# Batch 0's first pair of heads: later queries turned by DMA instead of by TensorE, with a new order of all steps

## The chip, the cores and the metric

The kernel runs on one core of a Trainium2 chip. Its engines work side by side, each through its own list of instructions in order: TensorE (PE in the profile; its weight loads are PEld), VectorE (DVE), ScalarE (ACT), GpSimd (POOL) and SyncE (SP), which issues DMA transfers. They wait for one another by semaphores. The metric is the device time of one execution in microseconds, as the median of the runs.

## The reference

Attention with routing, followed by a two-layer MLP. There are 4 batches, 8 heads, 768 positions and 64 columns to a head. Each query and each key is assigned to that one of its head's 16 centroids to which it has the greatest cosine. A query sees only the keys with its own centroid:

```python
q_assign = np.argmax(np.einsum('bhsd,hcd->bhsc', q_n, c_n), axis=-1)
k_assign = np.argmax(np.einsum('bhsd,hcd->bhsc', k_n, c_n), axis=-1)
mask = q_assign[:, :, :, None] == k_assign[:, :, None, :]
scores = scale * np.matmul(q, k.transpose(0, 1, 3, 2))
scores = np.where(mask, scores, -1000000000.0)
```

A softmax over the keys and a product with `v` follow. The heads are put side by side to rows of 512, and `x @ w_in` (to 2048), `h * sigmoid(h)` and `@ w_out` (back to 512) give the output, 3072 x 512 in float32.

## The kernel before

**Heads and tiles.** Heads are handled in pairs (`p` from 0 to 3), positions in six tiles of 128. Batch 0 runs in two rounds: the first two query tiles of all heads (`NA` = 2, 256 queries), then the other four (512 queries). Batches 1 to 3 run whole. The MLP runs in nine units (`mlp`): batch 0 in three of two tiles, the other batches in two of three tiles each.

**A part** (`part`, line 477 on) prepares tiles of queries and keys for the score matmul. Rows are rounded to fp16 (`hi`, lines 530 to 534) and the remainder kept as a second fp16 (`lo`, line 538). Then the tiles are turned, so that columns lie on partitions; TensorE multiplies them with the centroids (`logits`), the maximum is sought, and a 0/1 code of 16 columns marks the centroid. The code, turned as well, stands as 16 more rows under the 64 rows of values in the buffer `ab`. A score matmul (line 804) takes all 80 rows, so that masked scores come out far below the others.

There are two routes for a part. By TensorE (`turn` is a pair of engines): line 573 transposes values and remainders, 128 columns at once, eight tiles to a bank, and an engine evicts them to `lt` (lines 588, 590); logits take two matmuls to a tile (lines 618 and 622, `twin`); the code is compared out of the logits on VectorE (lines 668, 693), put next to the fp16 rows, transposed by line 573 once more (80 columns), and evicted to `ab` (lines 584, 586). By DMA (`turn` is "DMA"): SyncE issues a DMA transpose (line 553) straight into `ab`; logits take one matmul of 32 columns to a tile (line 627); VectorE adds the two halves (line 644) and finds the maximum (664), GpSimd subtracts it (676), VectorE marks (703, 705) and flips in blocks of 32 (718), and four copies, one for each group of 32 partitions, place the code in `ab` (line 735, `PUTB` names the engine for each group). In the kernel before all of batch 0 goes by TensorE, batches 1 to 3 go by DMA.

**Attention and MLP.** A head's scores go through the exponential on ScalarE (line 811), then line 832 multiplies with V (`vt`, cast by lines 418 to 422), and VectorE normalizes (845, 850). The result is transposed to `xt` by DMA (869) or by TensorE (880). The MLP's first matmul is line 910, tanh 916 on ScalarE, the gate 921 on VectorE, the second matmul 945, then an eviction to `ot` (958 on ScalarE, 960 on VectorE) and the store (963).

**The order.** Every piece of work is a `step` with an engine, a duration that the program assumes, what it depends on, the buffers it takes, and a key. `Plan.order` goes through the steps in assumed time: the step that can start earliest goes next, at equal times that with the lowest key. The outcome is the list of instructions of each engine. Assumed times only make the order; on the chip each instruction waits for the data that it needs. Numbers at the head of the kernel shape the keys and delays: `AT` gives the due times of the rounds and batches, `ML` those of the MLP units, `LEADS` how far ahead of its due time a part's key lies, `REST`, `RLOAD` and `SOON` after which head a part or a load may be placed, `PW` after which event a piece of the MLP's weights is fetched on GpSimd's queue, `DONE`, `WSL`, `FLIP` and `LATE` how much later than assumed something lands. `VC`, `TK`, `TQ`, `TR`, `TS`, `HI`, `HR`, `XT` and `EVAC` name the engine of a kind of work by pair, chunk or unit. Line 356 issues matmuls on zeros into assumed gaps of TensorE until the assumed time `UNREAD`, and up to `MORE` beyond a gap of over 400 ns.

Of the kernel before, what the change touches and what calls it, by code (L numbers as in the profile page):

```python
# [33 lines left out]
class Plan:  # L34
# [14 lines left out]
    def step(self, eng, w, fn, after=(), use=(), key=0.0, load=None, hold=0.0, pace=None, flip=False, lag=None, slack=0.0, port=False):  # L49
        s = Step()  # L50
        s.eng, s.w, s.fn, s.key, s.load, s.hold, s.flip = eng, w, fn, key, load, hold, flip
        s.lag = self.LAG.get(eng, 0) if lag is None else lag
        s.slack = slack
        s.port = port or eng == "POOL"
        s.use = list(use)
        s.n = len(self.steps)
        flat = []

        def gather(a):
            if isinstance(a, (list, tuple)):  # L60
                for x in a:
                    gather(x)
            elif a is not None:
                flat.append(a)

        gather(list(after))
        gather(pace)
        s.after = list({id(x): x for x in flat}.values())
        s.start = s.end = None
        for b in s.use:  # L70
            b.left += 1
        self.steps.append(s)
        return s
# [125 lines left out]
def kernel(  # L199
# [80 lines left out]
    def buf(name):  # L280
        return Buf(pools[name])
# [15 lines left out]

    SMALL = 30
    ISSUE = 470
    PW = [11, 5, 7, 13, 12, 27, 17, 2, 21, 10, 14, 19]  # L300
    UNREAD = 80000.0
    COLD = 8500.0
    MORE = 250.0
    LATE = 900
    FLIP = 1500
    DONE = 600
    WSL = 1000
    AT = [32.0, 63.0, 91.3, 118.4, 233.2, 272.8]
    ML = [55.5, 113.0, 73.2, 121.1, 198.2, 239.3, 267.5, 305.4, 257.3, 449.1]
    PUTB = ["POOL", "POOL", "POOL", "POOL"]  # L310
    VC = ["ACT", "ACT", "POOL", "ACT"]
    VB = "POOL"
    TK = ["ACT", "ACT", "DVE", "DVE", "DVE"]
    TQ = ["DVE", "ACT", "DVE", "DVE", "DVE"]
    TR = ["ACT", "DVE", "DVE", "DVE"]
    TS = ["ACT", "DVE", "DVE", "DVE"]
    HI = ["ACT", "ACT", "ACT", "POOL"]
    HR = ["DVE", "POOL", "DVE", "POOL"]
    LEADS = [27.5, 133.1, 361.9]
    REST = [3, 6, 3, 11]  # L320
    RLOAD = [2, 0, 3, 0]
    SOON = [7, 5, 7, 4]
    XT = ["DVE", "ACT", "ACT", "DVE"]
    EVAC = ["DVE", "DVE", "DVE", "ACT", "ACT", "ACT", "DVE", "ACT", "ACT", "ACT"]
    SPARE = 0
    FINE = 2

# [31 lines left out]

    plan.filler = (pools["M"], lambda t: 180.0 if t < COLD else 112.0, unread, UNREAD, MORE)  # L360

# [22 lines left out]
    def load_q(b, p, key, j0=0, j1=NJ, eng="SP", hs=(0, 1), pace=None):  # L384
        if (b, p) not in nqs:
            nqs[b, p] = buf("nq")
        x = nqs[b, p]

        def f():
            e = nc.sync if eng == "SP" else nc.scalar  # L390
            h0, h1 = 2 * p + hs[0], 2 * p + hs[-1] + 1
            e.dma_start(T["nq"][x.i][:, hs[0] : hs[-1] + 1, j0 * D : j1 * D], rows(q, b, h0, h1, j0, j1))

        s = step(eng, ISSUE, f, use=[x], key=key, load=110 * (j1 - j0) * len(hs), pace=pace, slack=LATE if b else 300 if eng == "ACT" else 0)
        for h in hs:
            for j in range(j0, j1):
                ld_q[b, p, h, j] = s
        return s
# [3 lines left out]
    def load_v(b, p, key, pace=None):  # L402
        eng = VC[p] if b == 0 else VB
        x = buf("nv")

        def f():
            nc.sync.dma_start(T["nv"][x.i], rows(v, b, 2 * p, 2 * p + 2, 0, NJ))

        s = step("SP", ISSUE, f, use=[x], key=key, load=1310, pace=pace, slack=LATE if b else 0)
        for h in range(2):  # L410
            y = buf("vt")
            vts[b, 2 * p + h] = y

            def g(h=h, y=y):
                dst = T["vt"][y.i][:, 0 : NJ * VW].rearrange("p (j c) -> p j c", c=VW)[:, :, 0:D]
                src = T["nv"][x.i][:, h, :].rearrange("p (j d) -> p j d", d=D)
                if eng == "ACT":
                    nc.scalar.copy(dst, src)
                else:
                    (nc.gpsimd if eng == "POOL" else nc.vector).tensor_copy(dst, src)  # L420

            w = {"POOL": pool_w(384), "ACT": act_w(384), "DVE": dve_w(384, 0.55)}[eng]

            cast_v[b, 2 * p + h] = step(eng, w, g, port=eng == "DVE", after=[s, s_ones], use=[x, y], key=key + 20)
# [52 lines left out]
    def part(b, p, segs, a0, due, lead=20.0, hi_eng="POOL", turn="DMA", twin=False, sub="POOL", code_eng=None, pace=None, wait=None):  # L477
# [238 lines left out]
        if turn == "DMA":  # L716
# [8 lines left out]
            for g in range(4):  # L725
# [14 lines left out]
                load = 10 * n if code_eng[g] == "SP" else None  # L740
                placed.append(step(code_eng[g], w, put, after=[s_flip, s_log], use=[ohT, A], key=key + 13 * span, load=load, port=code_eng[g] == "DVE", lag=Plan.LAG.get(code_eng[g], 0) + DONE))

# [229 lines left out]
    def weight(kind, n, event):  # L972

        x, use, name = event

        def f():
            nc.gpsimd.tensor_copy(pace, T[name][use.i][:, D : D + 1])
            if kind == "in":
                nc.gpsimd.dma_start(
                    win_s[:, :, ts(n, 512)], moe_w_in.rearrange("(r p) f -> p r f", p=128)[:, :, ts(n, 512)]  # L980
                )
            else:
                nc.gpsimd.dma_start(
                    wout_s[:, 2 * n : 2 * n + 2, :],
                    moe_w_out[256 * n : 256 * n + 256, :].rearrange("(c p) d -> p c d", p=128),
                )

        return step("POOL", 840, f, after=[x], use=[use], key=-1, load=2450 if kind == "in" else 1220, slack=WSL)


    want = {(n, h): AT[n] + (AT[n + 1] - AT[n]) * h / H for n in range(NU + B - 1) for h in range(H)}

# [13 lines left out]
    engines = dict(twin=True, sub="DVE")  # L1006
    for h in range(2):
        part(
            0, 0, [("k", h, 0, NJ), ("q", h, 0, NA)], (NJ + NA) * h, want[0, h], lead=LEADS[0], hi_eng=HI[0],
            turn=(TK[h], TQ[h]), wait=s_split if h else None, **engines,  # L1010
        )
    for p in range(1, NP):
        part(
            0, p, [("k", 0, 0, NJ), ("k", 1, 0, NJ), ("q", 0, 0, NA), ("q", 1, 0, NA)], 0, want[0, 2 * p], lead=LEADS[0],
            hi_eng=HI[p], turn=(TK[1 + p], TQ[1 + p]), wait=s_cent, **engines,
        )
# [3 lines left out]
    def at(place, f):  # L1020
        todo.setdefault(place, []).append(f)

    for p in range(NP):
        at(RLOAD[p], lambda s, p=p: load_q(0, p, want[1, 2 * p] - 30, NA, NJ, pace=s))
        at(
            REST[p],
            lambda s, p=p: part(
                0, p, [("q", 0, NA, NJ), ("q", 1, NA, NJ)], 2 * (NJ + NA), want[1, 2 * p], lead=LEADS[1], pace=s,
                hi_eng=HR[p], turn=(TR[p], TS[p]), **engines,
            ),  # L1030
        )
    for b in range(1, B):
        for p in range(NP):
# [3 lines left out]
            for f, early in ((load_k, 32), (load_q, 31), (load_v, 30)):  # L1037
                at(place - (SOON[0] if soon else SOON[1]), lambda s, b=b, p=p, f=f, due=due - early: f(b, p, due, pace=s))
            for i in range(2):
                at(  # L1040
                    place + i - (SOON[2] if soon else SOON[3]),
                    lambda s, b=b, p=p, i=i: part(
                        b, p, [("k", i, 0, NJ), ("q", i, 0, NJ)], 12 * i, want[b + NU - 1, 2 * p + i], lead=LEADS[2], pace=s, code_eng=PUTB
                    ),
                )
    for place in range(H * (B + NU - 1)):
        n, h = divmod(place, H)
        per = (AT[n + 1] - AT[n]) / H
        if n < NU:
# [7 lines left out]
    for n in range(4):  # L1057
        w_in_done.append(weight("in", n, events[PW[n]]))
    for n in range(8):
        w_out_done.append(weight("out", n, events[PW[4 + n]]))  # L1060
    units = [(0, *r) for r in UNITS] + [(b, 3 * c, 3 * c + 3) for b in range(1, B) for c in range(2)]
    for n, (b, j0, j1) in enumerate(units):
        mlp(b, j0, j1, ML[n], ML[n + 1], lambda t, n=n: EVAC[n], n == len(units) - 1)

# [31 lines left out]
```

## Time and profile before

| what | value |
|---|---|
| median of the runs | 304.36 us (304.25 to 304.38, 3 runs) |
| the profiled execution | 305.28 us, of it span 303.5 us |
| TensorE busy | 297.6 us |
| ScalarE busy | 226.2 us |
| VectorE busy | 196.6 us |
| GpSimd busy | 118.7 us |

Times in the profile are microseconds from the start of the span unless marked ns. A row of a group gives line, engine, operation, output and input, shapes, count, then busy time and mean of one, then the engine's idle time just before and who ended it. Busy times of groups overlap, since matmuls are pipelined: what a matmul costs on the engine is the distance between starts.

### The profile page before, as it was taken

The page shows a single profiled execution, that of the slowest core. Times are in us where ns is not written, and L with a number is a line of the kernel's source. Part 1 is how long each engine was busy: PE and PEld are TensorE (multiplying, and loading weights), DVE is VectorE, ACT ScalarE, POOL GpSimd, SP SyncE. Part 2 cuts the span into 40 slices and gives each one's busy share as a digit, 9 for nine tenths or more (in the row PEclk, how much of TensorE's full clock was granted, in tenths as well). Part 3 has the DMA queues.
Part 4 walks back from the last instruction along what each step waited for, and adds up shares of the span by engine and source line. Part 5 has one row for each costly group of instructions (what it writes and reads, how often), then busy time and mean ns, then how long its engine had stood idle before and what let it go on. Part 6 is the DMA issues. An engine that isn't in the chain of part 4 may idle for free.

```text
span 303.5 us, 8340 instructions
## 1 busy us (share of the span) xinstructions
PE 297.6 (98%) x3257; PEld 196.9 (65%) x3257; DVE 196.6 (65%) x484; ACT 226.2 (75%) x470; POOL 118.7 (39%) x242
## 2 busy tenths in 40 slices
PE   8999999999999999999999999999999999999995
PEld 6998777658867746666566655766656665555444
DVE  5999687888867946697567962688601686364020
ACT  5869999949899936988779867899888964253221
POOL 3346333497644677367377360464320000000000
PEclk9999999999999999999999999999999999999999
DMA  7999969977579966773968663854403000101211
GB/s 229 304 252 251 207 96 202 201 217 183 116 167 167 235 121 228 164 186 74 248 134 222 91 165 105 247 51 78 81 35 95 5 0 2 69 0 38 88 50 69
DMA packets 68695, 41.53 MB, mean 137 GB/s; under 512 B 48048, under 2 KB 65712, under 8 KB 68656
## 3 DMA queue, kind: packets, MB, share of 16 engines
q1 hardware_dynamic: 63952, 36.64, 50.4%
q0 software_dynamic: 4288, 4.20, 8.7%
q8 instruction: 25, 0.41, 0.6%
q10 hardware_dynamic: 416, 0.16, 0.2%
q14 instruction: 14, 0.11, 0.1%
HBM read 27.30 MB, written 6.29 MB: 111 GB/s over the span
## 4 chain that ended last, share of the span: by engine, by line
PE 94%; DMA 3%; ACT 1%; DVE 0%; issue 0%; ACTq 0%
PE bank L910 27%; PE bank L945 26%; PE bank L804 19%; PE bank L832 11%; PE bank L573 3%; DMA ab<-hl 3%; PE bank L627 2%; PE bank L356 2%; ACT P L811 1%; PE bank L618 1%; PE bank L622 1%; PE bank L880 1%; ACT lt L588 0%; DVE ot L960 0%; ACT ot L958 0%
## 5 line engine op out<-in xcount | busy, mean ns | idle before, releaser
L811 ACT ACTIVATE P<-bank 128x512 f16<-128x512 f32 x288 | 160.2, 650 | 25.7 <-PE bank L804 24.6
L945 PE MATMUL bank<-wout_s,gq 128*128 128x512 f16 (+1 forms) x400 | 100.2, 370 | 0.0
L910 PE MATMUL bank<-xt,win_s 128*128 128x384 f16 (+1 forms) x576 | 96.8, 308 | 0.0
L921 DVE SCALAR_TENSOR_TENSOR gq<-tn,bank 128x384 f16<-128x384 f32 (+1 forms) x144 | 69.4, 503 | 39.3 <-ACT tn L916 36.4
L804 PE MATMUL bank<-ab 80*128 80x256 f16 (+1 forms) x384 | 92.8, 326 | 0.0
L916 ACT ACTIVATE tn<-bank 128x384 f32<-128x384 f32 (+1 forms) x144 | 67.9, 498 | 24.1 <-PE bank L910 22.8
L910 PEld LDWEIGHTS <-win_s 128*128 128x128 f16 x576 | 54.7, 97 | 28.6
L735 POOL COPY ab<-ohT 16x384 f16<-16x384 f16 x96 | 51.5, 536 | 27.6 <-DVE ohT L718 13.5
L945 PEld LDWEIGHTS <-gq 128*128 128x128 f16 x400 | 37.3, 98 | 30.4
L832 PEld LDWEIGHTS <-P 128*128 128x128 f16 x1152 | 46.0, 97 | 12.0 <-ACT P L811 0.8
L832 PE MATMUL bank<-vt,P 128*128 128x65 f16 x1152 | 50.4, 193 | 0.6 <-ACT P L811 0.6
L804 PEld LDWEIGHTS <-ab 80*128 80x128 f16 x384 | 35.0, 97 | 21.9 <-issue 0.2
L676 POOL TENSOR_TENSOR Df<-L,mx 128x192 f32<-128x192 f32 x24 | 13.2, 549 | 40.7 <-DVE mx L664 37.7
L538 DVE SCALAR_TENSOR_TENSOR hl<-nk,hl 128x384 f16<-128x384 f32 (+1 forms) x29 | 19.2, 665 | 6.7 <-POOL hl L534 6.6
L958 ACT COPY ot<-bank 128x512 f32<-128x512 f32 (+1 forms) x16 | 8.9, 558 | 18.0 <-PE bank L945 17.9
L644 DVE TENSOR_REDUCE L<-bank 128x192 f32<-128x384 f32 x24 | 13.2, 551 | 13.4 <-PE bank L627 12.2
L538 DVE SCALAR_TENSOR_TENSOR hl<-nq,hl 128x384 f16<-128x384 f32 (+3 forms) x33 | 19.9, 602 | 0.9 <-POOL hl L534 0.9
L850 DVE TENSOR_TENSOR xn<-bank,rz 128x384 f16<-128x384 f32 (+2 forms) x40 | 19.0, 475 | 1.2
L845 DVE RECIPROCAL rz<-bank 128x6 f32<-128x6 f32 (+2 forms) x40 | 7.2, 180 | 17.1 <-PE bank L832 9.7
L534 POOL TENSOR_SCALAR hl<-nk 128x384 f16<-128x384 f32 (+1 forms) x25 | 13.8, 554 | 10.9 <-PE bank L573 8.7
L534 POOL TENSOR_SCALAR hl<-nq 128x384 f16<-128x384 f32 (+2 forms) x27 | 14.1, 524 | 1.5 <-DMA nq<-in_q_dram 1.4
L718 DVE STREAM_TRANSPOSE ohT<-oh 128x384 f16<-128x384 f16 x24 | 13.8, 576 | 0.8
(60 smaller groups left out, 180.6 us busy)
## 6 DMA issues: line engine op xcount, KB each, us to landing
nv<-in_v_dram SPq DMA_DIRECT2D x16, 384.0 KB, 5.4
out_dram<-ot SPq DMA_DIRECT2D x23, 256.0 KB, 2.1
nk<-in_k_dram SPq DMA_DIRECT2D x15, 384.0 KB, 4.2
nq<-in_q_dram SPq DMA_DIRECT2D x12, 384.0 KB, 4.6
wout_s<-in_moe_w_out_dram POOLq DMA_DIRECT2D x8, 256.0 KB, 7.0
win_s<-in_moe_w_in_dram POOLq DMA_DIRECT2D x4, 512.0 KB, 9.4
nq<-in_q_dram SPq DMA_DIRECT2D x4, 256.0 KB, 6.4
nk<-in_k_dram SPq DMA_DIRECT2D x2, 192.0 KB, 2.6
```

The costliest lines, as they stand in the source:

```text
L534: nc.gpsimd.tensor_scalar(out=dh, in0=src, scalar1=qs, scalar2=1.0, op0=ALU.mult, op1=ALU.mult)
L538: nc.vector.scalar_tensor_tensor(out=dl, in0=src, scalar=qs, in1=dh, op0=ALU.mult, op1=ALU.subtract)
L718: nc.vector.transpose(T["ohT"][ohT.i][:, 0:n, :].rearrange("p n c -> p (n c)"), T["oh"][oh.i][:, 0:n, :].rearrange("p n c -> p (n c)"),)
L735: nc.gpsimd.tensor_copy(dst, src)
L804: nc.tensor.matmul(banks[sb.i][:, at : at + 128 * (c1 - c0)], ab[0:80, kt[j], :], ab[0:80, qt + c0 : qt + c1, :].rearrange("p n c -> p (n ...
L811: nc.scalar.activation(out=T["P"][P.i][:, 0:at], in_=banks[sb.i][:, 0:at], func=AF.Exp, bias=0.0, scale=ESC if b else -ESC)
L832: nc.tensor.matmul(banks[O.i][:, (D + 1) * t : (D + 1) * t + nn], w, vt[:, VW * j : VW * j + nn], start=(j == 0), stop=(j == NJ - 1), skip ...
L850: nc.vector.tensor_tensor(out=T["xn"][xn.i][:, 0:nq, (h % 2) * D : (h % 2) * D + D], in0=banks[O.i][:, 0 : (D + 1) * nq].rearrange("p (t c ...
L910: nc.tensor.matmul(banks[bank.i][:, 0:n], win_s[:, r, ts(fb, 128)], T["xt"][xtb[b].i][:, r, 128 * j0 : 128 * j1], start=(r == 0), stop=(r ...
L916: nc.scalar.activation(out=T["tn"][tn.i][:, 0:n], in_=banks[bank.i][:, 0:n], func=AF.Tanh, bias=0.0, scale=1.0)
L921: nc.vector.scalar_tensor_tensor(out=T["gq"][g.i][:, fb % 4, 0:n], in0=T["tn"][tn.i][:, 0:n], scalar=1.0, in1=banks[bank.i][:, 0:n], op0=A ...
L945: nc.tensor.matmul(banks[bank.i][:, 0 : c1 - c0], T["gq"][gqs[fc // 4].i][:, fc % 4, ts(t, 128)], wout_s[:, fc, c0:c1], start=(fc == 0), s ...
```

## The change

The later 512 queries of batch 0's first pair of heads (8 tiles) go by the DMA route, as the parts of batches 1 to 3 do: `RT` chooses the route for each pair. Their code is placed by `PUTB`, as theirs is, and there the second partition group now goes by a DMA on SyncE's queue in all DMA-routed parts. All numbers that shape the order and most choices of engines are others. The zeros end at 45 us of assumed time and no longer go beyond a gap.

```diff
-    PW = [11, 5, 7, 13, 12, 27, 17, 2, 21, 10, 14, 19]
-    UNREAD = 80000.0
+    PW = [9, 6, 8, 11, 5, 26, 13, 2, 17, 4, 19, 22]
+    UNREAD = 45000.0
     COLD = 8500.0
-    MORE = 250.0
+    MORE = 0.0
     LATE = 900
     FLIP = 1500
-    DONE = 600
-    WSL = 1000
-    AT = [32.0, 63.0, 91.3, 118.4, 233.2, 272.8]
-    ML = [55.5, 113.0, 73.2, 121.1, 198.2, 239.3, 267.5, 305.4, 257.3, 449.1]
-    PUTB = ["POOL", "POOL", "POOL", "POOL"]
-    VC = ["ACT", "ACT", "POOL", "ACT"]
+    DONE = 400
+    WSL = 300
+    AT = [-10.9, 71.7, 88.1, 238.0, 366.9, 396.1]
+    ML = [-113.1, 222.5, 30.1, 200.9, 344.0, 390.7, 161.9, 493.0, 360.6, 591.5]
+    PUTB = ["POOL", "SP", "POOL", "POOL"]
+    VC = ["DVE", "POOL", "DVE", "POOL"]
     VB = "POOL"
-    TK = ["ACT", "ACT", "DVE", "DVE", "DVE"]
-    TQ = ["DVE", "ACT", "DVE", "DVE", "DVE"]
-    TR = ["ACT", "DVE", "DVE", "DVE"]
-    TS = ["ACT", "DVE", "DVE", "DVE"]
-    HI = ["ACT", "ACT", "ACT", "POOL"]
-    HR = ["DVE", "POOL", "DVE", "POOL"]
-    LEADS = [27.5, 133.1, 361.9]
-    REST = [3, 6, 3, 11]
-    RLOAD = [2, 0, 3, 0]
-    SOON = [7, 5, 7, 4]
+    TK = ["DVE", "ACT", "ACT", "DVE", "DVE"]
+    TQ = ["DVE", "ACT", "ACT", "ACT", "DVE"]
+    TR = ["DVE", "DVE", "DVE", "DVE"]
+    TS = ["ACT", "DVE", "ACT", "DVE"]
+    RT = ["DMA", "PE", "PE", "PE"]
+    HI = ["POOL", "ACT", "POOL", "ACT"]
+    HR = ["ACT", "DVE", "DVE", "DVE"]
+    LEADS = [459.5, 76.9, 362.1]
+    REST = [1, 2, 6, 12]
+    RLOAD = [0, 0, 0, 8]
+    SOON = [5, 5, 5, 5]
     XT = ["DVE", "ACT", "ACT", "DVE"]
-    EVAC = ["DVE", "DVE", "DVE", "ACT", "ACT", "ACT", "DVE", "ACT", "ACT", "ACT"]
+    EVAC = ["ACT", "DVE", "DVE", "ACT", "DVE", "ACT", "ACT", "ACT", "ACT", "ACT"]
...
                 0, p, [("q", 0, NA, NJ), ("q", 1, NA, NJ)], 2 * (NJ + NA), want[1, 2 * p], lead=LEADS[1], pace=s,
-                hi_eng=HR[p], turn=(TR[p], TS[p]), **engines,
+                hi_eng=HR[p], **(engines | dict(turn=(TR[p], TS[p])) if RT[p] == "PE" else dict(code_eng=PUTB)),
```

## The prediction

> **What bounds the kernel now.** I read the page's engine rows and slices first, to see which engine can be the bound.
>
> ```profile
> span 303.5 us, 8340 instructions
> PE 297.6 (98%) x3257; PEld 196.9 (65%) x3257; DVE 196.6 (65%) x484; ACT 226.2 (75%) x470; POOL 118.7 (39%) x242
> PEclk9999999999999999999999999999999999999999
> DMA  7999969977579966773968663854403000101211
> ```
>
> TensorE is busy for all but 5.9 us, at full clock; nothing else comes near. So the time is the sum of what TensorE is given, plus its idle. Where the idle lies, the busy time by stretch says (columns: stretch, length, then busy time and instructions of PE, PEld, DVE, ACT, POOL, then clock, DMA share, GB/s).
>
> ```profile
> 0.00:1.05 1.05, 0.00 (x1) 0.01 (x1) 0.23 (x2) 0.33 (x1) 0.40 (x8) 1.00 0.00 0
> 1.05:13.20 12.15, 12.14 (x160) 10.23 (x161) 9.22 (x32) 8.27 (x15) 2.80 (x16) 1.00 0.95 288
> 13.20:35.10 21.90, 21.16 (x401) 18.45 (x399) 20.62 (x58) 19.35 (x39) 11.41 (x23) 1.00 1.10 244
> 35.10:100.00 64.90, 64.78 (x836) 47.37 (x835) 49.91 (x133) 57.63 (x135) 36.87 (x70) 1.00 0.85 171
> 100.00:120.00 20.00, 19.43 (x200) 11.77 (x199) 14.19 (x35) 12.33 (x27) 14.02 (x27) 1.00 0.84 196
> 120.00:300.10 180.10, 180.08 (x1668) 109.05 (x1666) 102.48 (x227) 127.90 (x257) 53.17 (x103) 1.00 0.41 98
> 300.10:303.50 3.40, 0.00 (x0) 0.00 (x0) 0.00 (x0) 0.37 (x1) 0.00 (x0) 0.93 0.12 39
> ```
>
> 1.05 us go before the first matmul and 3.40 after the last (eviction, store, end); the change touches neither. Between them only 0.01 + 0.74 + 0.12 + 0.57 + 0.02 = 1.46 us are idle: 0.74 in the attention of batch 0's first queries, 0.57 around 100 to 120. A new order alone can win that and little more. One thing hides in the busy time: matmuls on zeros, which compute nothing (line 356). By form; then the same line's busy time in a stretch, which holds all 42; then the chain that ended last (start, length, what):
>
> ```profile
> L356 PE MATMUL bank<-zeros 128*128 128x256 f16 x42 | 7.8, 355 | 1.0 <-DVE zeros L334 1.0
> ```
>
> ```profile
> 0.00:13.30 13.30, 7.66 (x42) 5.11 (x42) 1.00 0.88 265
> ```
>
> ```profile
> 1.05 5.66 PE bank L356 x28
> 7.20 0.76 PE bank L356 x7
> 7.97 0.45 PE bank L573 x8
> 39.02 0.44 PE bank L910 x4
> 102.06 7.87 DMA ab<-hl
> 109.98 0.47 PE bank L627 x12
> 110.44 3.46 PE bank L945 x16
> ```
>
> 28 of the 42 run ahead of the first real matmul, the other 14 in early gaps (7 in 0.76 us, 109 ns each, so 1.5 us). The chain also gives the price of a transpose on TensorE: 0.45 / 8 = 56 ns. And the one sizeable wait later on is of the kind this change adds: logits (L627) held up until a DMA transpose, from 102.06 to 109.98, had landed; 0.57 us of TensorE idle came of it.
>
> **The change, part by part.** *The first pair's later queries leave TensorE.* Their 8 tiles of 128 queries were transposed twice there (values, then codes): 16 x 56 ns = 0.90 us gone. Their logits were 16 matmuls, two to a tile; by DMA it is one to a tile, 8. Starts of such matmuls, in order of time:
>
> ```profile
> 9.94 0.17 PE L618 MATMUL bank<-stk,lt 128*128 128x16 f16 x1
> 9.97 0.17 PE L622 MATMUL bank<-stk,lt 128*128 128x16 f16 x1
> 9.99 0.17 PE L618 MATMUL bank<-stk,lt 128*128 128x16 f16 x1
> ```
>
> They are 25 ns apart, so 8 x 25 = 0.20 us. Together TensorE does 1.10 us less. That is the change's surest term: in a stretch without idle it comes off the end in full.
>
> Here a page reads otherwise. "TensorE: Matmul & The Clock Gate" of the Trainium skill (Part 4: PE-mode transpose) puts a transpose at about 275 ns in one kernel's context. By that figure 16 of them would be an estimated 4.4 us, and the whole sum -5.1 where I come to -1.6. This trace has them start 56 ns apart, and the measurement decides.
>
> *What the DMA route costs elsewhere.* A transfer, a sum of logits, a peak, a subtraction on GpSimd, a mark, a flip, and four placings. The routed tiles of batches 1 to 3 show them, 12 tiles at a time against 8 here:
>
> ```profile
> L644 DVE TENSOR_REDUCE L<-bank 128x192 f32<-128x384 f32 x24 | 13.2, 551 | 13.4 <-PE bank L627 12.2
> L718 DVE STREAM_TRANSPOSE ohT<-oh 128x384 f16<-128x384 f16 x24 | 13.8, 576 | 0.8
> L735 POOL COPY ab<-ohT 16x384 f16<-16x384 f16 x96 | 51.5, 536 | 27.6 <-DVE ohT L718 13.5
> ```
>
> At 8/12 that is 0.37 + 0.38 us on VectorE, and the peak and mark about what the old route's took. So VectorE gains some 0.7 us of work here.
>
> *Work dealt out anew in the first 35 us.* VectorE is the fullest helper there (20.62 of 21.90 us above). The prices, of VectorE from 8 to 35 us, then of ScalarE from 2 to 35:
>
> ```profile
> L586 DVE TENSOR_SCALAR ab<-bank,gain 80x1024 f16<-80x1024 f16 x9 | 6.5, 740 | 0.8 <-PE bank L573 0.5 <-ACT P L811 0.3
> L590 DVE COPY lt<-bank 128x1024 f16<-128x1024 f16 x8 | 5.2, 680 | 0.0
> L532 DVE TENSOR_SCALAR hl<-nq 128x512 f16<-128x512 f32 x2 | 0.8, 414 | 0.0
> ```
>
> ```profile
> L588 ACT COPY lt<-bank 128x1024 f16<-128x1024 f16 x3 | 3.1, 1022 | 0.3 <-PE bank L573 0.3
> L418 ACT CAST vt<-nv 128x384 f16<-128x384 f32 x6 | 2.8, 509 | 2.2 <-DMA nv<-in_v_dram 2.2
> L584 ACT ACTIVATE ab<-bank,gain 80x1024 f16<-80x1024 f16 x2 | 2.3, 1143 | 0.0
> L530 ACT ACTIVATE hl<-nk 128x768 f16<-128x768 f32 x2 | 1.7, 844 | 1.7 <-DMA nk<-in_k_dram 1.0 <-PE bank L573 0.7
> ```
>
> VectorE: head 0's first eviction comes (+0.68), pair 1's two go (-1.36); four of the second kind, pairs 1 and 2, go (-2.96), and one of the later queries of pair 2 (-0.74); the V casts of pairs 0 and 2 come, four in all (no VectorE row; 384 columns against L532's 512 at 0.41, so 0.31 to 0.41 each, +1.4); the rounding of later queries leaves for pair 0 and comes for pairs 1 and 3 (+0.41); the DMA route +0.7. Sum: -1.9 us. ScalarE: evictions -1.02 + 2.04 + 4.57 (four of L584) + 1.14 (pair 2's later ones), the first pair's later ones -1.02 - 1.14, six casts -2.8, rounding of pair 0's first rows -1.1 (1024 columns at 0.844 / 768, moved to GpSimd) and of its later rows +0.6, pairs 2 and 3 changing places: +1.2. So from 13.2 to 35.1 the two would stand near 18.7 and 20.5 us of 21.9, where they stood at 20.6 and 19.4. The 0.74 us of TensorE idle there should shrink; I take off 0.7 of the 1.46 us between first and last matmul, and leave the rest as waits of the new order. Bounds: +0 to -1.46 without a new wait.
>
> *Placing by SyncE's queue.* For one of the four partition groups the placing moves from GpSimd to a DMA, in all 25 routed parts. GpSimd is spared 24 x 0.54 = 13 us that nobody waits for at 39% busy. Landing times of small transfers (median us) and SyncE's longest queue wait for the helper ahead of a transpose (total us, times, longest):
>
> ```profile
> out_dram<-ot SPq DMA_DIRECT2D x2, 128.0 KB, 1.7
> ab<-hl SPq DMA_TRANSPOSE x24, 4.3
> SPq L553 <- DVE hl L538: 42.0, 15, 5.7
> ```
>
> The placing lands between 1.7 us (nearest: the smallest transfer, and like this one issued by SyncE) and 4.3 us after its issue. Four copies on GpSimd took 4 x 0.54 = 2.1 us, so a part is ready between 0.4 us earlier and 2.2 us later than before. Behind the placing in SyncE's queue stand the next transposes and loads, which now wait for the flip too. What covers it, from GpSimd's and TensorE's rows:
>
> ```profile
> 60.34 3.22 POOL L735 COPY ab<-ohT 16x384 f16<-16x384 f16 x6 [1.09 <-DVE ohT L718]
> ```
>
> ```profile
> 64.21 1.96 PE bank L804 x12
> ```
>
> The first part's four copies end near 62.5, its scores begin at 64.21: 1.7 us of cover in the tightest place, and TensorE has other matmuls to do there if the order gives it any. I charge 0.2 us (bounds 0 and 2.2).
>
> *Loads, parts and weights moved.* Loads and parts of batch 1's first two pairs are placed two heads later (7 to 5), those of the rest near where they were; weights are asked for after other events, some earlier, some later, on GpSimd's queue, where the rounding of pairs 0 and 2 and the V casts of pairs 1 and 3 now stand among them and would wait with it; GpSimd, at 11.41 of 21.90 us, has room for that. Later parts are covered by batch 0's MLP, still undone at 35 us: 192 matmuls of line 910 with 256 columns at 0.44 / 4 = 0.11 us and 96 of line 945 at 3.46 / 16 = 0.216, 42 us of TensorE. ScalarE's later exponentials fit into 180 us of which it uses 128. Charged nothing; without that cover each us is a us.
>
> *Fillers.* The rule for zeros ends at 45 instead of 80 us and no longer overfills a gap; the last one ran before 13.3 us anyway. No term.
>
> Sum: -1.1 - 0.7 + 0.2 = -1.6 us. The profiled execution took 305.28 us (span 303.5 and 1.78 around it); the runs' median is 304.36, 0.9 less. Taken from the median: 302.8 us.
>
> **The rivals.** *TensorE waits for the first pair's DMA turn* (slower). It is issued while DMA is at a share of 1.10. The first turns of batch 1 show what a loaded queue does:
>
> ```profile
> L553 SPq DMA_TRANSPOSE ab<-hl x4: 1273/2220/2854, 44.7 to 57.0; - x4
> DMA to landing us min/median/max: 3.8/5.9/8.6
> ```
>
> If the order counts on the median of 4.3 us and the turn takes 8.6, TensorE, which works in order, stands 4.3 us at the logits: 302.8 + 4.3 = 307.1. It decides from 2.2 us of wait on. For it: the stall at 102 to 109.98. Against: pairs 1 to 3 stay on TensorE and can go first.
>
> *Head of line on SyncE* (slower). A placing waits for a late flip, the transposes behind it come late, and a part's scores with them. If the new order has used up the 1.7 us of cover, and batch 1's first two parts come 2.2 us late each: 302.8 - 0.2 + 4.4 = 307.0; it decides from 2.2 us of TensorE's waiting in all. Against: the parts after the first two need not be so tight, and SyncE stands waiting for VectorE ahead of transposes for 42 us already.
>
> *The idle only moves* (no change): TensorE does 1.1 us less, and the new order waits 1.1 us in other places: 304.4.
>
> *The clock falls.* The fillers before 6 us ran at 5.66 / 28 = 202 ns, later ones at 109: the array starts at half speed, and no gap in this trace is long enough to show it fall back. If the 4.3 us wait stood there unfilled and the next 3.4 us ran at half speed, 1.7 us more: 308.8. "TensorE: Matmul & The Clock Gate" of the Trainium skill (What's actually happening) names an idle window of about 3.4 us as what halves the clock; no run here shows it.
>
> **How the numbers follow.** Chances: the forecast 0.53, no change 0.12, the wait for the turn 0.17, SyncE's queue 0.13, the clock 0.05. A measurement of this kernel can tell about 0.2%, 0.6 us, from no change. So faster 0.53, within 0.12, slower 0.35. The likeliest case alone spans 301.2 (1.1 us less work, all 1.46 us of idle and 0.6 of the 1.5 us of zeros in gaps won) to 303.7. The range for all goes from 301.2 to 307.1, and leaves out the clock's case, half of the waits over 4.3 us, and little below.
>
> **What would show it.** Right: transposes on TensorE fall by 16, L618 and L622 by 8 each, L627 rises by 8; TensorE's idle from 13 to 35 us is under 0.74 us; the span falls by 1 to 2 us. Wrong: a wait of over 1 us at L627 or L804 on the first pair, or a gap in TensorE between 60 and 75 us for batch 1's first parts; GpSimd's busy time not falling by some 10 us; zeros in other numbers.

## The result and the profile after

The changed kernel takes 311.76 us (311.22 to 312.05, 5 runs) against 304.38 us (304.25 to 305.37): 1.0228 times as long, 95% interval 1.0207 to 1.0249. It is 7.4 us slower. The profiled execution took 311.86 us, its span is 309.8 us. Lines below the `RT` list have moved down by one: the logits of the DMA route are line 628, the DMA transpose is line 554, scores are 805, the MLP's matmuls 911 and 946.

The page of the profile after, the rows that answer to those of before:

```profile
span 309.8 us, 8372 instructions
PE 299.7 (97%) x3233; PEld 197.6 (64%) x3233; DVE 198.5 (64%) x483; ACT 229.3 (74%) x467; POOL 111.5 (36%) x226
PEclk9999579999999999999999999999999999999999
DMA  7999974999859989692759784453301101000211
```

TensorE has 24 matmuls fewer (16 transposes, and 8 logits for 16), and is busy longer. In the fifth and sixth slices, from 31 to 46 us, the clock was not full. The busy time by stretch shows the place:

```profile
1.05:13.20 12.15, 11.39 (x151) 9.43 (x152) 9.55 (x33) 6.22 (x8) 5.55 (x21) 1.00 0.93 278
13.20:30.10 16.90, 16.55 (x333) 15.27 (x329) 15.29 (x47) 16.90 (x32) 8.90 (x18) 1.00 1.19 194
30.10:33.90 3.80, 0.19 (x5) 0.06 (x3) 0.94 (x2) 0.90 (x2) 0.00 (x0) 0.78 1.41 130
33.90:45.00 11.10, 11.10 (x93) 8.07 (x94) 5.08 (x16) 7.68 (x17) 2.72 (x7) 0.61 0.88 207
45.00:100.00 55.00, 55.00 (x719) 39.15 (x718) 44.09 (x114) 50.27 (x112) 30.77 (x57) 1.00 0.84 177
100.00:120.00 20.00, 19.47 (x244) 13.67 (x242) 17.02 (x42) 18.62 (x42) 12.36 (x22) 1.00 0.87 178
120.00:306.10 186.10, 185.95 (x1707) 111.98 (x1704) 106.34 (x233) 127.82 (x259) 50.81 (x95) 1.00 0.42 103
306.10:309.80 3.70, 0.00 (x0) 0.00 (x0) 0.00 (x0) 0.59 (x1) 0.00 (x0) 0.85 0.19 71
```

The spans differ by 6.3 us, and the rows add up to that (the profiled execution of the kernel before took 0.9 us more than its median, so the medians lie further apart). Idle between the first and the last matmul went from 1.46 to 5.40 us (0.76 + 0.35 + 3.61 + 0.53 + 0.15): +3.9. The tail grew by 0.3. Busy time grew by 2.1 although 1.1 us of work is gone, so the work left took about 3.2 us longer; the stretch at a clock of 0.61 is the only one with matmuls below full clock.

What TensorE waited for (us in total, times, longest; 0.5 us of the first row are another part's turn between 100 and 120 us), the two matmul groups around the wait, and the turn in the chain that ended last:

```profile
PE bank L628 <- DMA ab<-hl: 4.1, 2, 3.6
PE bank L619 <- DVE lt L591: 0.4, 1, 0.4
PE bank L805 <- DVE ab L587: 0.3, 1, 0.3
PE bank L805 <- ACT ab L585: 0.2, 1, 0.2
```

```profile
29.62 0.62 PE L574 MATMUL bank<-ident,hl 128*128 128x128 f16 x8
33.85 0.40 PE L628 MATMUL bank<-stk,ab 128*128 128x32 f16 x8 [3.61 <-DMA ab<-hl]
```

```profile
20.70 13.10 DMA ab<-hl
```

The new DMA turn was issued at 20.70 us and landed 13.1 us later. TensorE came to its logits 3.6 us too early and stood there. The DMA rows of 15 to 36 us, of after and then of before, show the other side:

```profile
DMA packets 4220, 3.56 MB, mean 170 GB/s; under 512 B 1185, under 2 KB 4215, under 8 KB 4215
q0 software_dynamic: 2505, 2.48, 89.1%
win_s<-in_moe_w_in_dram POOLq DMA_DIRECT2D x4, 512.0 KB, 11.5
ab<-hl SPq DMA_TRANSPOSE x1, 13.1
```

```profile
DMA packets 4515, 5.01 MB, mean 238 GB/s; under 512 B 199, under 2 KB 4510, under 8 KB 4510
```

In the same 21 us DMA, busy nearly throughout in both, moved 3.56 MB where it moved 5.01. (1.15 MB of the difference are three loads of 384 KB on SyncE's queue that the kernel before issues there at 17 to 18 us and the changed one at 38 to 40, so the two stretches are not alike; plain_copy below compares like with like.) About a thousand small packets came with the turn. Six pieces of MLP weight were on their way on GpSimd's queue while the turn was.

### The profile page after: what moved, and what is told of

Read it like the earlier page. It is cut to its first block, busy times and chain, and to the rows that moved or that the text cites. A ratio compares the mean times of both kernels' runs of the same rounds, so it can differ in the third digit from the quotient of the medians.

```text
span 309.8 us, 8372 instructions
## 1 busy us (share of the span) xinstructions
PE 299.7 (97%) x3233; PEld 197.6 (64%) x3233; DVE 198.5 (64%) x483; ACT 229.3 (74%) x467; POOL 111.5 (36%) x226
## 4 chain that ended last, share of the span: by engine, by line
PE 86%; DMA 7%; DVE 4%; issue 1%; POOL 1%; ACT 0%; DVEq 0%; ACTq 0%
PE bank L911 27%; PE bank L946 26%; PE bank L805 19%; PE bank L833 10%; DMA ab<-hl 6%; PE bank L628 2%; DVE hl L539 1%; DVE lt L591 1%; DMA craw<-in_centroids_dram 1%; PE bank L574 1%; PE bank L881 1%; DVE mx L669 0%; DVE hl L694 0%; POOL hl L535 0%; POOL cy L437 0%
## 5 line engine op out<-in xcount | busy, mean ns | idle before, releaser
L812 ACT ACTIVATE P<-bank 128x512 f16<-128x512 f32 x288 | 152.6, 637 | 18.4 <-PE bank L805 16.1
L946 PE MATMUL bank<-wout_s,gq 128*128 128x512 f16 (+1 forms) x400 | 98.5, 370 | 0.1
L911 PE MATMUL bank<-xt,win_s 128*128 128x384 f16 (+1 forms) x576 | 92.7, 312 | 0.0
L805 PE MATMUL bank<-ab 80*128 80x256 f16 (+1 forms) x384 | 90.9, 330 | 0.7 <-DVE ab L587 0.3
L917 ACT ACTIVATE tn<-bank 128x384 f32<-128x384 f32 (+1 forms) x144 | 66.0, 473 | 20.1 <-PE bank L911 15.4
L736 POOL COPY ab<-ohT 16x384 f16<-16x384 f16 (+1 forms) x75 | 39.7, 529 | 24.9 <-PE bank L805 8.6
L805 PEld LDWEIGHTS <-ab 80*128 80x128 f16 x384 | 34.5, 98 | 21.6 <-issue 0.7
L677 POOL TENSOR_TENSOR Df<-L,mx 128x192 f32<-128x192 f32 (+1 forms) x25 | 14.2, 567 | 47.8 <-DVE mx L665 46.1
L645 DVE TENSOR_REDUCE L<-bank 128x192 f32<-128x384 f32 (+1 forms) x25 | 13.6, 543 | 12.2 <-PE bank L628 10.5
L421 POOL CAST vt<-nv 128x384 f16<-128x384 f32 x28 | 15.6, 584 | 0.4
L628 PEld LDWEIGHTS <-ab 128*128 128x128 f16 x296 | 10.7, 96 | 7.8 <-DMA ab<-hl 4.6
## 6 DMA issues: line engine op xcount, KB each, us to landing
win_s<-in_moe_w_in_dram POOLq DMA_DIRECT2D x4, 512.0 KB, 11.5
```

What stands on the lines that cost most here:

```text
L628: nc.tensor.matmul(banks[Lb.i][:, 32 * t : 32 * t + WN], w, stk[:, hh, 0:WN], start=True, stop=True)
L736: nc.gpsimd.tensor_copy(dst, src)
L805: nc.tensor.matmul(banks[sb.i][:, at : at + 128 * (c1 - c0)], ab[0:80, kt[j], :], ab[0:80, qt + c0 : qt + c1, :].rearrange("p n c -> p (n ...
L812: nc.scalar.activation(out=T["P"][P.i][:, 0:at], in_=banks[sb.i][:, 0:at], func=AF.Exp, bias=0.0, scale=ESC if b else -ESC)
L911: nc.tensor.matmul(banks[bank.i][:, 0:n], win_s[:, r, ts(fb, 128)], T["xt"][xtb[b].i][:, r, 128 * j0 : 128 * j1], start=(r == 0), stop=(r ...
L917: nc.scalar.activation(out=T["tn"][tn.i][:, 0:n], in_=banks[bank.i][:, 0:n], func=AF.Tanh, bias=0.0, scale=1.0)
```

## The experiments

Ratios are to the kernel before, run on the same chip beside each. Diffs are to the changed kernel unless said otherwise. Where numbers of the order are changed, the whole order is made anew from them; where only what a step issues is changed, the order stays. weights_after_place and the late runs keep TensorE's list but for what they move; in SyncE's list they also let loads come earlier, as told there.

### Undoing the route alone

```diff
-    RT = ["DMA", "PE", "PE", "PE"]
+    RT = ["PE", "PE", "PE", "PE"]
```

> The first pair's later queries go by TensorE again; all other numbers of the changed kernel stay, and the order is made from them. Theory A (the 3.6 us wait of the logits for the DMA turn, and the half clock that follows it from 32 to 42 us, are the whole loss): no wait at 30 us, clock full throughout, 1.1 us more work; 311.8 - 3.8 - 3.2 + 1.1 = about 306, within 1.5. Theory B (the rest of the new order, engines and loads, loses the time, and the turn is only where it shows): another wait of some microseconds between 20 and 45 us, 309 or more.

314.79 us, ratio 1.0337 (1.0284 to 1.0390). The wait at 30 us is gone and the clock stays full, and yet it is slower still. The waits of TensorE are others (5.4 us of idle between 45 and 100 us), and the pieces of the first MLP weight land in 7.9 us (median):

```profile
PE bank L946 <- DMA wout_s<-in_moe_w_out_dram: 1.8, 1, 1.8
PE bank L911 <- DVE xt L888: 1.1, 1, 1.1
```

So the numbers of the changed kernel do not give a good order for another program. Theory A as I put it (the wait and the clock are the whole loss) fell: removing them by a new order brings other waits. The time is the one that I gave for theory B, though its waits do not stand at 20 to 45 us. With a whole order made anew, this run cannot tell what the turn costs in the order of the changed kernel.

### An order that expects the turn late

```diff
-            turned = [step("SP", 120 * n, turn_dma, ..., flip=True, slack=FLIP)]
+            turned = [step("SP", 120 * n, turn_dma, ..., flip=True, slack=FLIP if b else 9000)]
```

> The changed kernel with one assumed time raised: batch 0's DMA turn is taken to land 9.0 us late in place of 1.5, so that the order puts other matmuls ahead of its logits. Theory A: the wait and the half clock go, and the 1.1 us of work stay saved: about 304 (302.5 to 305.5). Theory B: waits at other places in the first 60 us, 308 or more.

319.11 us, ratio 1.0444 (1.0401 to 1.0487): theory B's side (308 or more, waits in the first 60 us), and far beyond its bound. The order now has the MLP's first matmuls ahead, and these wait for their weights:

```profile
PE bank L911 <- DMA win_s<-in_moe_w_in_dram: 4.2, 1, 4.2
PE bank L574 <- DVE hl L539: 1.4, 1, 1.4
```

### A smaller change of the order's numbers, in the kernel before

```diff
-    DONE = 600
-    WSL = 1000
+    DONE = 400
+    WSL = 300
```

> The kernel before with two assumed delays smaller (DONE 400 for 600, WSL 300 for 1000), no other change; the order is made anew from them. If an order made from numbers not fitted to it loses microseconds by itself: 306 or more, by waits in other places. If the order is not sensitive: 304 to 305.

306.74 us, ratio 1.0070 (1.0043 to 1.0098), as expected of a sensitive order. Two assumed delays, with no other change, cost 2.3 us. A comparison of orders made anew can be off by that much for reasons of the order alone, so in the next runs I kept the order and changed single steps.

### Zeros in the wait

Order kept. Just ahead of the logits of the first pair's later queries:

```diff
+            if b == 0 and turn == "DMA":
+                for _ in range(34):
+                    nc.tensor.matmul(banks[Lb.i][:, 0:256], zeros[:, 0:128], zeros, start=True, stop=True)
```

> The changed kernel in its own order, with 34 matmuls on zeros (34 x 109 ns = 3.7 us) put right ahead of the first pair's logits, where TensorE stands idle. Theory A with the clock as a cost of its own: the wait stays, the clock stays full, and the cold stretch from 33.9 to 42.5 us runs at full rate: about 3 us less, 308.5 (307.5 to 309.5). If the clock costs nothing beyond the wait: 311.8 or a little more.

311.18 us, ratio 1.0198 (1.0168 to 1.0227); against 1.0228 the intervals overlap. The clock did stay full. Two stretches of this run:

```profile
33.90:45.00 11.10, 11.10 (x127) 9.16 (x125) 8.06 (x25) 10.04 (x26) 3.03 (x7) 1.00 0.95 217
45.00:100.00 55.00, 52.79 (x705) 37.01 (x703) 41.56 (x107) 48.06 (x104) 31.38 (x58) 1.00 0.87 185
```

Up to 45 us 127 matmuls ran where after ran 93. But from 45 to 100 us TensorE is now idle for 2.2 us, where after had none: 0.9 us for ScalarE (row L815), 0.7 for GpSimd (L739) and 0.6 for a piece of the second weight. A TensorE that is faster there comes too early for others. So the half clock cost about 3 us where it was. Of these the medians show 0.6 us at the end; the intervals would allow for none and for 2 or more. (The zeros ran 0.7 us past the turn's landing, which takes a little from the gain.)

### Less weight to fetch

Order kept; only a quarter of the first MLP weight is fetched, and each of its matmuls takes that quarter.

```diff
-                    win_s[:, :, ts(n, 512)], moe_w_in.rearrange("(r p) f -> p r f", p=128)[:, :, ts(n, 512)]
+                    win_s[:, 0:1, ts(n, 512)], moe_w_in.rearrange("(r p) f -> p r f", p=128)[:, 0:1, ts(n, 512)]
...
-                        banks[bank.i][:, 0:n], win_s[:, r, ts(fb, 128)], ...
+                        banks[bank.i][:, 0:n], win_s[:, 0, ts(fb, 128)], ...
```

> The changed kernel in its own order; of each of the four pieces of the first MLP weight only a quarter is fetched (0.5 MB in place of 2 MB, the other rows are not used: the first MLP matmul takes the same quarter four times). If the weight loads on GpSimd's queue make the turn slow: it lands in 5 to 8 us in place of 13.1, the wait falls under 1 us, the clock stays full, about 305 (304 to 306.5). If the turn is slow by itself or by something else: landing over 11 us, 311 or more.

305.99 us, ratio 1.0031 (1.0016 to 1.0045). Landing times in `ab` from 15 to 40 us (the longest is the turn), and what TensorE waited for later on:

```profile
DMA to landing us min/median/max: 2.0/3.5/4.9
```

```profile
PE bank L628 <- DMA ab<-hl: 1.1, 1, 1.1
PE bank L805 <- DMA ab<-ohT: 1.0, 1, 1.0
```

With 1.5 MB less beside it the turn lands in 4.9 us in place of 13.1, no wait stands at 30 us, and the clock is full. The first row is a turn of batch 1, at 104 us. The second row is the placing by SyncE that I had among the rivals: 1.0 us at 61 us.

### Is it the turning, or any transfer there?

Order and weights kept; the 8 tiles are copied by a plain transfer of the same bytes (so these queries are not turned, and their rows of the result are not attention's).

```diff
-                nc.sync.dma_start_transpose(T["ab"][A.i][:, a0 : a0 + n, :], src)
+                if b:
+                    nc.sync.dma_start_transpose(T["ab"][A.i][:, a0 : a0 + n, :], src)
+                else:
+                    nc.sync.dma_start(T["ab"][A.i][:, a0 : a0 + n, :], src.rearrange("p (n c) -> p n c", c=pitch))
```

> The changed kernel in its own order; the first pair's 8 tiles are copied to the same place by a plain transfer of the same 0.25 MB in place of a DMA transpose (so those queries are not turned, and their rows of the result are not attention's). If it is the turning, with its many small packets, that suffers beside the weight loads: the copy lands in under 7 us, the weights land in 8 to 9 us, no wait over 1 us at the logits, 305 to 307. If any transfer there is as slow: 10 us or more, and 310 or more.

305.93 us, ratio 1.0024 (1.0000 to 1.0048). The copy and the first weight in this run:

```profile
ab<-hl SPq DMA_DIRECT2D x1, 256.0 KB, 6.7
win_s<-in_moe_w_in_dram POOLq DMA_DIRECT2D x4, 512.0 KB, 8.9
```

The same bytes, at the same place, beside the same loads, land in 6.7 us, and the weights in 8.9 in place of 11.5. So it is the turning that delays itself and them; whether by its small packets or by the turning as such, the run does not tell. This run shows two things more: 5.8 us of the 7.4 hang on it, and even with a cheap transfer the changed kernel is not faster than before.

### The weights after the turn

Order kept on TensorE; the two of the first weight's four pieces that the MLP takes last are fetched only when the turn has landed, the other two first.

```diff
+                m = (2, 0, 1, 3)[n]
+                if m >= 2:
+                    held_back.append(lambda: fetch(m))
+                    return
...
+            if b == 0 and turn == "DMA":
+                nc.gpsimd.tensor_copy(paced[0:64], T["ab"][A.i][0:64, a0, 0:1])
+                for go in held_back:
+                    go()
```

> The changed kernel with TensorE's order untouched; the first two issues of first-MLP weight fetch columns 0 to 1023, and the two pieces with the later columns are issued only once the first pair's DMA turn has landed. All bytes are fetched. Theory W (the turn and the weight loads on GpSimd's queue slow one another; the wait that follows is the largest part of the loss): the turn lands in 7 to 9.5 us, no wait over 1 us at the logits, clock full, about 305.5 (304.5 to 307). Rival (the turn is slow whatever is fetched beside it, or the weights are then late for the MLP): a wait of 3 us or more at 30 or at 36 to 42 us, 309 or more.

307.90 us, ratio 1.0104 (1.0072 to 1.0136). The turn lands in 10.2 us, TensorE waits 0.7 us for it and 0.9 for the second weight. All bytes are fetched, and half of the loss is gone: between my two expectations.

The same with the second group placed by GpSimd (in `put`, the DMA becomes a copy by GpSimd where it stood):

> As weights_after_turn, with the second group's placing done by GpSimd at the place in the order where SyncE's issue stood, in all 25 parts. If the placing by SyncE costs TensorE the wait of 1.0 us that the run with less weight showed: 0.7 to 1.5 us less than weights_after_turn, near 304.5. If it costs nothing: the same within 0.5 us, or more by what GpSimd's 13 us bring.

309.16 us, ratio 1.0155 (1.0129 to 1.0180): not faster, and by the medians 1.3 us slower. The waits are again at the weights:

```profile
PE bank L916 <- DMA win_s<-in_moe_w_in_dram: 2.7, 2, 2.1
```

This edit changes one thing more. In SyncE's list, batch 1's first loads of keys, queries and values stand behind the first pair's placing, which waits for the turn. With the placing gone from that list, the loads are issued at 22 to 26 us, among the weights, where weights_after_turn issues them at 36 to 37.

### The logits later, all else kept

TensorE's order kept but for one chain: the 8 logits and what follows them up to the placing stand about 4 us of assumed time later, behind the matmuls that came next.

```diff
+    chain = {"logits": 4010, "total": 3710, "peak": 4050, "below": 4050, "mark": 4050, "flip": 4050, "put": 4050}
...
+    for s in moved[1:]:
+        s.start += chain[s.fn.__name__]
+    order.sort(key=lambda s: (s.start, s.n))
```

> The changed kernel with one step put elsewhere by hand: the 8 logits matmuls of the first pair's later queries, and what follows them up to the placing, stand behind 55 other matmuls that were next in TensorE's list; the rest of the order is as it was. The loads and the turn stay as they are. Theory W, sharpened (the turn takes 13 us beside the weight loads, and the order puts TensorE in front of it 4 us early although its codes are used only later): the turn still lands near 33.8, the wait shrinks below 0.5 us, the clock stays full, 304 to 305.5. If those steps are needed so early, or the weights are then waited for: 307 or more.

312.47 us, ratio 1.0247 (1.0210 to 1.0284): nothing won. The waits of TensorE:

```profile
PE bank L911 <- DMA win_s<-in_moe_w_in_dram: 6.0, 1, 6.0
PE bank L628 <- DMA ab<-hl: 0.6, 1, 0.6
```

The wait for the first pair's turn is gone (the second row is a later part's turn, at 111 us). A wait of 6.0 us for the first weight took its place, again with a half clock. Before the run I had written that the loads stay as they are; they did not. The placing is one of the steps that moved, and in SyncE's list three loads of 384 KB for batch 1 came ahead of it. SyncE's rows (start, length), of after and then of late_logits:

```profile
37.73 0.75 SPq L732 DMA_DIRECT2D ab<-ohT  x1
38.53 0.58 SPq L378 DMA_DIRECT2D nk<-in_k_dram  x1
```

```profile
22.92 0.58 SPq L378 DMA_DIRECT2D nk<-in_k_dram  x1
44.97 0.75 SPq L732 DMA_DIRECT2D ab<-ohT  x1
```

The piece that the MLP takes first landed 11.7 us after its issue in after, at 35.1 us, and 15.8 us after it here, at 39.8. The turn itself took 12.6 us, no longer than before. So most of the 6.0 us came in with the edit. Some of it was there in after, hidden by the wait for the turn: plain_copy comes to the same matmul at 33.6 us, which leaves an estimated 1.5 us. The runs that follow, and turn_late and weights_after_place above, have these loads early too.

late_logits again, with the pieces of both weights fetched in the order in which the MLP takes them:

```diff
+        n = (2, 0, 1, 3)[n] if kind == "in" else (2, 7, 3, 0, 4, 1, 5, 6)[n]
```

> As late_logits, and the pieces of both MLP weights are fetched in the order in which the MLP takes them, at the same times (in after, later pieces come first). If weights that land late cost anything once the wait is gone: 0.5 to 1.5 us less than late_logits; if they do not: the same within 0.5 us.

308.59 us, ratio 1.0146 (1.0109 to 1.0183), 3.9 us less: the wait for the first weight is 1.7 us, and none stands at the first pair's logits. The gain is larger than I had put down for it.

With SyncE's placing given to GpSimd in late_logits:

> As late_logits, with the second group's placing by GpSimd at the place in the order where SyncE's issue stood, in all 25 parts. If SyncE's placing makes TensorE wait once the turn's wait is gone (1.0 us in the run with less weight): 0.5 to 1 us less than late_logits; if its cost is hidden: the same within 0.5 us.

312.94 us, ratio 1.0279 (1.0254 to 1.0305): within 0.5 us of late_logits. Who places costs nothing that shows beside such waits (5.4 us for the first weight).

Last, late_remap with two pieces of the second weight held back until the turn has landed:

```diff
+            if kind == "out" and n in (1, 2) and not late:
+                held_back.append(f)
+                return
...
```

> As late_remap (the logits later, weight pieces in the order of their use), and two pieces of the second MLP weight, needed only after 50 us, are issued once the turn has landed. With 0.5 MB less beside it the turn lands in 8 to 11 us and the first MLP weight earlier: the wait for it (1.7 us in late_remap) falls under 0.7 us; 305.5 to 307.5. If it does not, the turn and the first weight alone are too much for the stretch: 308 or more.

This one is unclear: one run of six took 306.34 us, the others 312.87 to 314.79, among them the profiled one, in which the turn took 12.1 us and TensorE stood 4.2 us for nothing that the profile shows:

```profile
34.76 0.58 PE L810 MATMUL bank<-ab 80*128 80x512 f16 x1 [4.19 <-issue]
```

Neither expectation can be judged by it.

### The route alone, in the kernel before

```diff
+    RT = ["DMA", "PE", "PE", "PE"]
...
-                hi_eng=HR[p], turn=(TR[p], TS[p]), **engines,
+                hi_eng=HR[p], **(engines | dict(turn=(TR[p], TS[p])) if RT[p] == "PE" else dict(code_eng=PUTB)),
```

> The kernel before with the one change of route: the first pair's later queries by DMA, placed by GpSimd, all numbers as before, the order made anew from them. Theory W: the turn, issued among the weight loads, lands in 8 us or more, and TensorE waits for it or for weights that it delays; 306 to 312. If the route costs nothing in this order: 1.1 us less than before, 303 to 304.5.

Four runs of 313.92 to 321.79 us, spread too widely for a ratio. The turn was issued at 24.1 us and took 8.5; TensorE waited 2.1 us for it, with a half clock after that, so it was late here too. Batch 1's first loads were issued right behind the turn, at 25 to 28 us. How much of the rest is the route and how much an order not fitted to it stays open.

## Why the prediction was wrong

I forecast 302.8 us, with 301.2 to 307.1 as the range and 0.53 on faster. It came out at 311.76.

**The work taken off TensorE** came as counted: 24 matmuls fewer. **The idle up to 30 us**, from which I took 0.7 us off, did not shrink. From 13.2 to 30.1 us it went from 0.74 to 0.35 us, but from 1.05 to 13.2 it rose from 0.01 to 0.76, where TensorE waited for evictions by VectorE (rows L619 and L805 above); together 1.11 us where there were 0.75. This term failed by itself, and it is the rival of the idle that only moves. ScalarE, which I put at 20.5 of 21.9 us, was busy in every moment from 13.2 to 30.1 (16.90 of 16.90): I had its load too low, and 0.2 us of TensorE's waiting came of it there.

**The step that failed**, the one that decided, is the price of the first pair's turn. In "the change, part by part" I listed it as "a transfer" and charged its helpers, but not its time. In the rivals I bounded it by batch 1's first turns, 3.8 to 8.6 us, the nearest rows I saw. Those ran beside one weight load (the last was issued at 46.5 us); the new one stood beside six. It measured 13.1 us. And I had only asked who waits for the turn, not what the turn does to the loads beside it: the pieces of the first MLP weight took 11.5 us (median), where they land in 8.9 in plain_copy and landed in 9.4 before, in another order. With the wait for the turn out of the way they would have stopped TensorE for an estimated 1.5 us (under late_logits). I charged the weights nothing, with "batch 0's MLP" as cover for everything else; that MLP cannot start without them. The weight before, and its last fetches (the final numbers are the first and the last start):

```profile
win_s<-in_moe_w_in_dram POOLq DMA_DIRECT2D x4, 512.0 KB, 9.4
L983 POOL DMA_DIRECT2D wout_s<-in_moe_w_out_dram x8: 698/713/953, 7.1 to 46.5; - x8
```

**The likeliest case** should have been the rival that I gave 0.17, the wait for the turn. I had priced it at 4.3 us of idle; it was 3.6. That the two are close is luck: the turn took 13.1 us where I had 8.6, and TensorE came to it 9.5 us after its issue where I had 4.3. **The clock**, the rival with 0.05, came on top of it. I had it at 3.4 us of work at half speed and 1.7 us lost; it was 8.6 us and about 3 lost at that place, though the run with zeros won only 0.6 of them back by the medians.

**SyncE's queue** made TensorE wait nowhere in after. A wait of 1.0 us for its placing is there once the turn's wait is gone (less_weight). What I had as its harm, loads that stand behind a late placing, kept 1.15 MB out of the full stretch. **GpSimd** went down by 7.2 us, not 10. **A new order's own cost** stood in the sum as nothing: two margins are worth 2.3 us. Of the 7.4 us, 5.8 hang on the turn (plain_copy). The other 1.6 us are smaller than what a change of two margins does to the order; that no order with this route is faster than before was not shown.

## What to carry to other kernels

A transfer moved into a stretch where DMA is full has two prices: its own time there, and what it does to the transfers beside it. Take its price from a row with the same loads in flight, not from the median of the quiet ones, and ask of each load beside it who waits for it next. When a step is placed later by hand, look in every queue that it leaves: what stood behind it moves up. Here three loads did, and the experiment no longer compared what it was made to compare.

## What the runs showed of the hardware

**A DMA transpose beside software-queue loads.** 0.25 MB took 4.9 us with a quarter of the first weight beside it and 13.1 with all of it (8.5 in before_dma, another order); a plain copy of the same bytes in the same place took 6.7. Three loads more, issued behind it on SyncE's own queue, left it at 12.1 to 12.9 us (turn_late and the four late runs). The weight loads lost as well: 11.5 us with the turn, 8.9 with the copy, 7.9 with neither (undo_route, another order). The "DMA: Bandwidth & Descriptors" page of the Trainium skill (Rules for kernel authors) says that a transpose next to ordinary DMAs needs nothing. That stands in a rule on transfers that must wait for one another lest they corrupt data, and says nothing of time; by these runs it costs time.

**The clock.** In after it fell 2.0 us into the wait, and stayed at half for 10.2 us, 8.6 of them with TensorE busy throughout:

```profile
30.10:32.20 2.10, 0.14 (x3) 0.00 (x0) 0.94 (x2) 0.90 (x2) 0.00 (x0) 1.00 1.61 97
32.20:33.90 1.70, 0.05 (x2) 0.06 (x3) 0.00 (x0) 0.00 (x0) 0.00 (x0) 0.51 1.17 170
33.90:42.50 8.60, 8.60 (x70) 5.84 (x71) 3.39 (x11) 5.23 (x11) 1.58 (x4) 0.50 0.94 197
42.50:45.00 2.50, 2.50 (x25) 2.24 (x24) 1.69 (x5) 2.45 (x8) 1.14 (x3) 1.00 0.68 242
```

In the run with the route alone a wait of 2.1 us was enough, and half speed lasted 3.1 us after it:

```profile
32.60:35.70 3.10, 3.10 (x44) 2.73 (x45) 2.46 (x8) 0.00 (x0) 0.40 (x1) 0.50 1.15 268
```

In turn_late the clock held through a wait of 4.2 us and fell 0.7 us behind it, with TensorE at work; in late_logits it fell 3.5 us into a wait of 6.0:

```profile
33.20:37.70 4.50, 0.30 (x3) 0.02 (x1) 0.00 (x0) 1.28 (x2) 0.00 (x0) 1.00 1.16 266
38.40:41.80 3.40, 3.40 (x18) 2.41 (x17) 2.02 (x5) 2.37 (x7) 1.16 (x3) 0.50 0.85 181
```

```profile
37.40:39.80 2.40, 0.00 (x0) 0.00 (x0) 0.00 (x0) 0.00 (x0) 0.00 (x0) 0.51 1.16 272
39.80:44.30 4.50, 4.44 (x29) 3.22 (x30) 1.94 (x7) 2.00 (x5) 0.58 (x2) 0.50 0.53 95
```

So the length of a wait alone does not say whether or when the clock falls. The length of the half speed has a pattern. Summed from the granted clock in steps of 0.1 us it is 3.4 us in before_dma and turn_late, 6.8 in late_logits, late_place and late_hold, and 10.2 in after: one, two or three times 3.41 us.

"TensorE: Matmul & The Clock Gate" of the Trainium skill (What's actually happening) names some 3.4 us, of idling for the fall and of work for the rise. The steps of 3.41 us agree with that length. But in after and before_dma the clock fell after 2.0 and 1.8 us of idling, and in after it took 8.6 us of work to rise; why one rise took one such step and another three stays open.
